# Adaptive-LN mixer kernel: four modulation rows as two pairs in 32-column strips of TensorE

## The chip, the cores and the metric

One core of one Trainium2 chip runs the whole program. The metric is the device time of one execution in microseconds; a time given for a kernel is the median of several runs. The profile is of one execution of its own, and its times count from the first instruction.

## The reference, cut to what matters

A token mixer (a 2-D real FFT filter) and a channel MLP, each behind a layer norm that a condition vector `c` modulates, and the whole backward pass:

```python
mod = (silu(c) @ w_mod).reshape(1, 6, 1, 1024)
sa, ca, ga, sb, cb, gb = six rows of mod
h = layernorm(x) * (1 + ca) + sa
x = x + ga * A(h, w_r, w_i)            # irfft2(rfft2(h) * (w_r + i w_i))
h = layernorm(x) * (1 + cb) + sb
x = x + gb * B(h, w1, b1, w2, b2)      # layernorm, 1024 -> 3584, gelu, 3584 -> 1024
outputs: x, and the gradients of A_x, w_r, w_i, w1, b1, w2, b2, c, w_mod for a given grad_out
```

`x` and `grad_out` are 2048 tokens of 1024 (bf16), `w_mod` is 1024 x 6144. The six rows of `mod` are what the change touches: row 0 is `sa`, 1 `ca`, 2 `ga`, 3 `sb`, 4 `cb`, 5 `gb`.

## The kernel before, in words

The program is written with a framework that places instructions on the engines, puts each engine's instructions into one fixed order by priorities and an estimate of their times, and adds the semaphores. An engine then works strictly in that order. Program order is the base of the priorities, so work written later is drawn forward as filler where an engine would otherwise stand, as far as its inputs are there. `tc.issue_after(ins)` makes what is written in its block follow `ins` on the same engine; `tc.high_priority()` puts evictions of PSUM first; `nc.any.tensor_copy` lets the framework choose ScalarE or VectorE.

**Modulation rows.** `u_b` (L255) holds silu(c), each of its 1024 values repeated over 128 columns. `mod_block(r, h)` (L272) makes one half (512 columns) of row r: it loads a tile `wblk` of w_mod of 1 MB (128 partitions x 8 pieces of 512 columns, L270, on SyncE's DMA queue), runs eight matmuls of 128x128 weights from `u_b` with 128x512 of `wblk` (L278) into one PSUM buffer, and copies the result, which then stands in all 128 partitions alike, to the row's place in SBUF (L281). For rows 1 and 4 it adds 1 (L283). The tiles go round a ring of three (`mod_tile`, L264, tags px3, px4, px5). PSUM has two buffers of the tag "s" (`ps_s`), two of "d" (`ps_d`) and four of "f" (`ps_f`); mod_block takes from "s".

**Order around the rows.** Row 1 and row 5 come first, their loads between those of x and grad_out (L358 to L374). Row 5 becomes the columns `gb_col` through eight tiny matmuls (L378), and scales grad_out while it is transposed by TensorE (L386) into `gBoT` (L390 VectorE, L394 ScalarE). Row 0 follows (L780), then the making of the Fourier matrices (`gen_mats`), and the fold of row 0 into `saf` (L791, L792). Then come six early "ph blocks": `ph_part(fc, ...)` (L802) makes one of 28 blocks of grad_out @ w2.T, in 32 matmuls (L808), copies them out (L814) and stores them (L816). Its weights come transposed through `load_w2t` (L340) into two slots of `wt`. Rows 2, 3 and 4 are placed behind the fourth and the sixth early ph block, three half rows each (`late_mods`, L819 to L827).

VectorE and ScalarE meanwhile normalize x, multiply it by row 1 and fold it into `fbuf` (L829 to L846; `saf` is added in L846). The forward spectral part (`spectral_core`, L867) starts with matmuls L535 on `fbuf`. Its last step `consume_fwd` (L851) uses rows 2, 3 and 4 and stores the inputs of the MLP. The other 22 ph blocks are written behind the spectral part (L883) and serve it as filler. Then z blocks (L937, the first MLP layer and gelu) and b passes (L994, the second layer) follow in a plan written out by hand (L1030), then the backward pass. Two forms used elsewhere are named by the prediction: `strip_sum` (L216), sums over partitions with 32-column weights into one of four 32-partition strips of a PSUM buffer, and L983, four matmuls with one row each at partitions 0, 32, 64 and 96 with `tile_position`.

The change's diff has no other function; the pair temporaries of the spectral part use px2 to px5 after the ring has ended.

Of the kernel before, what the change touches and what calls it, by code (L numbers as in the profile page):

```python
# [11 lines left out]
BF16 = mybir.dt.bfloat16  # L12
# [5 lines left out]
P = 128  # L18
S = 2048
D = 1024  # L20
F = 3584
NT = S // P
NDC = D // P
NFC = F // P
KH = D // 2
# [10 lines left out]
def kernel(  # L36
# [24 lines left out]
    nc = tc.nc  # L61
# [11 lines left out]
    def ps_s(name):  # L73
        return psum.tile([P, 512], FP32, tag="s", name=name)
# [185 lines left out]
    sar = reg.tile([P, 2, 1, D], BF16, name="sar", tag="gm")  # L260
# [3 lines left out]
    def mod_tile():  # L264
        wring[0] += 1
        return reg.tile([P, NDC, KH], BF16, name="wblk", tag=PXT[3 + wring[0] % 3])

    def mod_load(r, h, wblk, eng):
        cb = 2 * r + h
        eng.dma_start(out=wblk, in_=w_mod[:, cb * KH:(cb + 1) * KH].rearrange("(j p) n -> p j n", p=P))  # L270

    def mod_block(r, h, wblk=None):  # L272
        if wblk is None:
            wblk = mod_tile()[:]
            mod_load(r, h, wblk, nc.sync)
        pm = ps_s("pm")
        for jc in range(NDC):
            nc.tensor.matmul(pm[:], lhsT=u_b[:, jc, :], rhs=wblk[:, jc, :], start=(jc == 0), stop=(jc == NDC - 1))  # L278
        dst = MOD_DST[r][:, h * KH:(h + 1) * KH]
        with tc.high_priority():  # L280
            nc.any.tensor_copy(out=dst, in_=pm[:])  # L281
        if r in (1, 4):
            nc.vector.tensor_scalar(out=dst, in0=dst, scalar1=1.0, scalar2=None, op0=ALU.add)  # L283

# [67 lines left out]
    wm = {}  # L352

    def mod_get(r, h):
        wm[r, h] = mod_tile()
        mod_load(r, h, wm[r, h][:], nc.sync)
# [14 lines left out]
    for h in range(2):  # L371
        mod_block(5, h, wm[5, h][:])
# [407 lines left out]
    for h in range(2):  # L780
        mod_block(0, h)
# [769 lines left out]
```

## Time and profile before

| | before |
|---|---|
| median of 3 runs | 1419.12 us (1417.3 to 1419.79) |
| span of the profiled execution | 1417.4 us; its own time isn't given apart, the span lies 1.7 us below the median |
| TensorE busy | 1367.5 us, 96%, 6839 matmuls in the records |
| VectorE busy | 1071.1 us, 76% |
| ScalarE busy | 745.6 us, 53% |
| GpSimd busy | 377.1 us, 27% |
| moved by DMA | 333.22 MB, mean 235 GB/s |
| modulation rows | 12 half rows, 93 of 96 matmuls in the records, 6.2 to 104 us |

How to read it: busy time of TensorE is the time in which a matmul is under way; matmuls overlap, so a single one lasts about 0.38 us and the next can start 0.22 us after it. What an engine cost at a place is therefore read from the start of one thing to the start of the next. A line in a view is named by its line of the kernel and by the tiles that it writes and reads (`pm<-wblk,u_b`). Idle time has the name of what ended it. A few records of matmuls are missing, so counts can be short by one or two.

### The profile page before, as it was taken

To read this page: it belongs to the slowest core of one execution; us is meant where nothing else is said; L and a number is where in the kernel's file an instruction comes from. 1 tells how busy PE (TensorE), PEld (TensorE's weight loads), DVE (VectorE), ACT (ScalarE), POOL (GpSimd) and SP (SyncE) were. 2 spreads that over 40 slices of the span, in tenths; PEclk is the share of its full clock that TensorE was granted. 3 is DMA by queue.
4 is the path that set the end of the run, shared out by engine and by line. 5 is a ranking of instruction groups with operands and counts; after the bars stand their busy time and mean duration, and the time that the engine had idled before them with its cause. 6 is when DMAs were issued, how large, how long until landed. Compare 5 with 4: busy or idle time off the path is not lost. (4 is left out here: it accounts for less than half of the span.)

```text
span 1417.4 us, 18569 instructions
## 1 busy us (share of the span) xinstructions
PE 1367.5 (96%) x6839; PEld 663.0 (47%) x6963; DVE 1071.1 (76%) x1503; ACT 745.6 (53%) x1063; POOL 377.1 (27%) x479
## 2 busy tenths in 40 slices
PE   5999999999999999999999999999999999999998
PEld 2545675444444444444444444344544565444443
DVE  5898889987698877886520788999488659898642
ACT  4775667667887765666315583343623445343211
POOL 5500623201112122212210011011367432322332
PEclk8899999999999999999999999999999999999999
DMA  9972647899688776687999399996699997666993
GB/s 330 304 226 72 181 137 226 261 277 348 239 235 267 231 252 233 200 275 232 292 287 233 115 271 319 210 298 193 191 279 281 242 242 207 189 180 182 288 261 118
DMA packets 356689, 333.22 MB, mean 235 GB/s; under 512 B 207578, under 2 KB 297200, under 8 KB 356470
## 3 DMA queue, kind: packets, MB, share of 16 engines
q1 hardware_dynamic: 319110, 205.61, 55.1%
q0 software_dynamic: 37488, 126.42, 25.7%
q8 instruction: 54, 0.88, 0.3%
q14 instruction: 37, 0.30, 0.1%
HBM read 166.77 MB, written 115.92 MB: 199 GB/s over the span
## 5 line engine op out<-in xcount | busy, mean ns | idle before, releaser
L808 PE MATMUL pp<-gBoT,wt 128*128 128x512 bf16 x874 | 196.3, 381 | 4.0 <-DMA wt<-in_B_w_dram 2.8
L1094 PE MATMUL pg<-w1T,gzr 128*128 128x512 bf16 x877 | 195.0, 379 | 3.7 <-ACT gn3b L1109 1.7
L1445 PE MATMUL gw1acc<-gzh,n3n 128*128 128x512 bf16 x877 | 194.1, 379 | 1.0
L1094 PEld LDWEIGHTS <-gzr 128*128 128x128 bf16 x896 | 86.4, 98 | 110.8 <-issue 7.9
L808 PEld LDWEIGHTS <-wt 128*128 128x128 bf16 x896 | 87.6, 98 | 107.5 <-DMA wt<-in_B_w_dram 3.3
L937 PEld LDWEIGHTS <-w 128*128 128x128 bf16 x896 | 87.1, 98 | 107.4 <-issue 2.7
L1445 PEld LDWEIGHTS <-n3n 128*128 128x128 bf16 x896 | 87.2, 98 | 105.2 <-issue 1.3
L937 PE MATMUL pz<-n3Ta,w 128*128 128x512 bf16 x439 | 98.2, 379 | 1.8 <-ACT gt L940 1.3
L937 PE MATMUL pz<-n3Tb,w 128*128 128x512 bf16 x436 | 98.0, 379 | 0.7 <-issue 0.2
L940 ACT ACTIVATE gt<-pz,b_col 128x512 bf16<-128x512 f32 x112 | 73.5, 684 | 38.1 <-PE pz L937 37.6
L994 PEld LDWEIGHTS <-hhA 128*128 128x128 bf16 x608 | 58.9, 98 | 73.4 <-issue 3.0
L1227 PE MATMUL gw2acc<-gB,hhsA 128*128 128x512 bf16 x406 | 91.2, 379 | 0.5
L1449 ACT CAST gwo<-gw1acc 128x512 bf16<-128x512 f32 x49 | 28.5, 582 | 111.0 <-PE gw1acc L1445 103.2
L194 DVE TENSOR_TENSOR gt<-gt,gt 128x2048 bf16<-128x2048 bf16 x56 | 68.5, 1224 | 20.6 <-ACT gt L953 19.4
L951 ACT ACTIVATE gt<-gt 128x2048 bf16<-128x2048 bf16 x28 | 53.5, 1910 | 55.1 <-DVE gt L194 55.1
L194 DVE TENSOR_TENSOR ct<-ct 128x2048 bf16<-128x2048 bf16 x68 | 80.8, 1217 | 1.4 <-DMA d_n<-ct 0.5
L1234 ACT CAST gwo<-gw2acc 128x512 bf16<-128x512 f32 x46 | 26.7, 582 | 101.0 <-PE gw2acc L1227 83.2
L1227 PEld LDWEIGHTS <-hhsA 128*128 128x128 bf16 x416 | 40.6, 98 | 47.9
L947 ACT ACTIVATE gt<-gt 128x2048 bf16<-128x2048 bf16 x28 | 53.5, 1910 | 1.7 <-DVE w2sA L194 1.0
L1450 POOL DMA_DIRECT2D out_dram<-gwo x56 | 30.7, 549 | 88.6 <-ACT gwo L1449 66.2
L953 ACT ACTIVATE gt<-gt 128x2048 bf16<-128x2048 bf16 x28 | 53.4, 1908 | 0.4
L814 ACT CAST pho<-pp 128x512 bf16<-128x512 f32 x59 | 33.5, 582 | 32.4 <-PE pp L808 31.9
(346 smaller groups left out, 2544.5 us busy)
## 6 DMA issues: line engine op xcount, KB each, us to landing
gzr<-d_gz SPq DMA_DIRECT2D x28, 512.0 KB, 6.4
wblk<-in_w_mod_dram SPq DMA_DIRECT2D x12, 1024.0 KB, 8.8
out_dram<-otl POOLq DMA_DIRECT2D x48, 256.0 KB, 4.5
out_dram<-gwo POOLq DMA_DIRECT2D x96, 128.0 KB, 4.2
d_ph<-pho POOLq DMA_DIRECT2D x21, 512.0 KB, 5.6
d_hh<-hhA POOLq DMA_DIRECT2D x19, 512.0 KB, 5.0
w<-in_B_w_dram SPq DMA_DIRECT2D x7, 1024.0 KB, 11.7
hhC<-d_ph SPq DMA_DIRECT2D x14, 512.0 KB, 9.5
```

Of the source, the lines that this page charges most:

```text
L194: return nc.vector.tensor_tensor(out=out, in0=a, in1=b, op=op)
L808: last_pe[0] = nc.tensor.matmul(pp[:], lhsT=wt[:, fg % 2, cch, k * P:(k + 1) * P], rhs=gBoT[j][:, cch, :], start=(cch == 0), stop=(cch == ...
L814: nc.any.tensor_copy(out=ov, in_=pv)
L937: last_pe[0] = nc.tensor.matmul(pz[:], lhsT=w1s[g][:, cch, k * P:(k + 1) * P], rhs=n3T[:, cch, :], start=(cch == 0), stop=(cch == NDC - 1))
L940: z_in = nc.scalar.activation(out=zb[:, k, :], in_=pz[:], func=ACT.Identity, bias=b1_col[:, fc:fc + 1], scale=1.0)
L947: nc.scalar.activation(out=av, in_=zb, func=ACT.Square)
L951: nc.scalar.activation(out=sg, in_=bv, func=ACT.Sigmoid, scale=2.0 * GK)
L953: nc.scalar.activation(out=bv, in_=bv, func=ACT.Sigmoid, scale=-2.0 * GK)
L994: last_pe[0] = nc.tensor.matmul(pbs[i][:], lhsT=hh[:, k, i * P:(i + 1) * P], rhs=wp[:, k, :], start=False, stop=(g == 6 and k == 3))
L1094: last_pg[0] = nc.tensor.matmul(pgs[i][:], lhsT=gzs[b, g][:, k, i * P:(i + 1) * P], rhs=w1Ts[g][:, k, h * KH:(h + 1) * KH], start=(g == 0 ...
L1227: nc.tensor.matmul(acc[:], lhsT=hh_of(fc)[:, t, :], rhs=gBs[t // 4][:, t % 4, h * KH:(h + 1) * KH], start=(t == 0), stop=(t == NT - 1))
L1445: nc.tensor.matmul(acc[:], lhsT=n3ns[t // 4][:, t % 4, cch * P:(cch + 1) * P], rhs=gz2[t // 8][:, t % 8, :], start=(t == 0), stop=(t == NT ...
```

## The change

Rows 1 and 5 are made from two loads of a whole row each, now one for each half of the 1024 contraction rows (`mod_get(r, jh)`, 4 pieces of 1024 columns per partition), and use two PSUM buffers at once (`mod_row`); their matmuls are as many and as large as before.

Rows 0 and 2, and rows 3 and 4, are made as pairs (`mod_pair`). The weights are 32 columns of `u_b`, and the four half rows of a pair are accumulated in the four 32-partition strips of one PSUM buffer: 4 strips x 8 contraction blocks of 128x512. The buffer is copied to `strips` in SBUF, then four matmuls with a weight of one row of ones (at partitions 0, 32, 64 and 96) spread each strip's first row to all 128 partitions, into four PSUM buffers ("d", "d", "s", "s"), which are copied to the rows' places as before. Row 2 moves from behind the early ph blocks to the place of row 0; rows 3 and 4 stand behind the fourth early ph block, none behind the sixth. The ring of three tiles stays, and a pair loads four tiles, two for each half of the contraction.

```diff
-    sar = reg.tile([P, 2, 1, D], BF16, name="sar", tag="gm")
+    sar = reg.tile([P, 3, 1, D], BF16, name="sar", tag="gm")
+    strips = sar[:, 2, 0, :]
...
-    def mod_tile():
-    def mod_load(r, h, wblk, eng):
-    def mod_block(r, h, wblk=None):
+    def mod_get(r, jh):
         wring[0] += 1
+        wblk = reg.tile([P, 4, D], BF16, name="wblk", tag=PXT[3 + wring[0] % 3])
+        nc.sync.dma_start(out=wblk[:], in_=w_mod[jh * KH:(jh + 1) * KH, r * D:(r + 1) * D].rearrange("(j p) n -> p j n", p=P))
+        return wblk
+
+    def mod_out(r, h, pm):
         dst = MOD_DST[r][:, h * KH:(h + 1) * KH]
         with tc.high_priority():
             nc.any.tensor_copy(out=dst, in_=pm[:])
         if r in (1, 4):
             nc.vector.tensor_scalar(out=dst, in0=dst, scalar1=1.0, scalar2=None, op0=ALU.add)
+
+    def mod_row(r, wblks):
+        pms = [ps_s("pm") for _ in range(2)]
+        for jh in range(2):
+            for h in range(2):
+                for j in range(4):
+                    nc.tensor.matmul(pms[h][:], lhsT=u_b[:, 4 * jh + j, :], rhs=wblks[jh][:, j, h * KH:(h + 1) * KH],
+                                     start=(jh == 0 and j == 0), stop=(jh == 1 and j == 3))
+        for h in range(2):
+            mod_out(r, h, pms[h])
+
+    def mod_pair(n, rows):
+        pm = ps_s("pm")
+        for jh in range(2):
+            wblks = [mod_get(r, jh) for r in rows]
+            for j in range(4):
+                for k in range(4):
+                    nc.tensor.matmul(pm[32 * k:32 * (k + 1), :], lhsT=u_b[:, 4 * jh + j, 0:32],
+                                     rhs=wblks[k // 2][:, j, k % 2 * KH:(k % 2 + 1) * KH],
+                                     start=(jh == 0 and j == 0), stop=(jh == 1 and j == 3))
+        row4 = strips[:, n * KH:(n + 1) * KH]
+        with tc.high_priority():
+            nc.any.tensor_copy(out=row4, in_=pm[:])
+        pbs = [(ps_d, ps_s)[k // 2]("pmb") for k in range(4)]
+        for k in range(4):
+            nc.tensor.matmul(pbs[k][:], lhsT=ones_bf[32 * k:32 * k + 1, :], rhs=row4[32 * k:32 * k + 1, :], start=True, stop=True,
+                             tile_position=(32 * k, 0))
+        for k in range(4):
+            mod_out(rows[k // 2], k % 2, pbs[k])
...
-    mod_get(1, 0)
+    wm1 = [mod_get(1, 0)]
     load_tok(x4s[0], A_x, 0)
-    mod_get(1, 1)
-    mod_get(5, 0)
-    for h in range(2):
-        mod_block(1, h, wm[1, h][:])
-    mod_get(5, 1)
+    wm1.append(mod_get(1, 1))
+    wm5 = [mod_get(5, 0)]
+    mod_row(1, wm1)
+    wm5.append(mod_get(5, 1))
...
-    for h in range(2):
-        mod_block(5, h, wm[5, h][:])
+    mod_row(5, wm5)
...
-    for h in range(2):
-        mod_block(0, h)
+    mod_pair(0, (0, 2))
     gen_mats()
...
-    late_mods = [(r, h) for r in (2, 3, 4) for h in range(2)]
     for fc in range(PH_EARLY):
         ph_part(fc, (0, 1, 2, 3))
         if fc % 2 == 1:
             load_w2t(fc // 2 + 2)
-            if fc > 1:
+            if fc == 3:
                 with tc.issue_after(last_pe[0].ins):
-                    for r, h in late_mods[3 * (fc // 2 - 1):3 * (fc // 2)]:
-                        mod_block(r, h)
+                    mod_pair(1, (3, 4))
```

More of the change, by code (lines that the diff above doesn't have):

```diff
@@ L259 @@
     sb_row, saf = sb_saf[:, 0, :], sb_saf[:, 1, :]
-    sar = reg.tile([P, 2, 1, D], BF16, name="sar", tag="gm")
+    sar = reg.tile([P, 3, 1, D], BF16, name="sar", tag="gm")
+    strips = sar[:, 2, 0, :]
     MOD_DST = {0: sar[:, 0, 0, :], 1: opca_row, 2: ga_row, 3: sb_row, 4: opcb_row, 5: gb_row}
     wring = [0]
-    def mod_tile():
+    def mod_get(r, jh):
         wring[0] += 1
-        return reg.tile([P, NDC, KH], BF16, name="wblk", tag=PXT[3 + wring[0] % 3])
-    def mod_load(r, h, wblk, eng):
-        cb = 2 * r + h
-        eng.dma_start(out=wblk, in_=w_mod[:, cb * KH:(cb + 1) * KH].rearrange("(j p) n -> p j n", p=P))
-    def mod_block(r, h, wblk=None):
[L273 to L278, printed above, removed]
+        wblk = reg.tile([P, 4, D], BF16, name="wblk", tag=PXT[3 + wring[0] % 3])
+        nc.sync.dma_start(out=wblk[:], in_=w_mod[jh * KH:(jh + 1) * KH, r * D:(r + 1) * D].rearrange("(j p) n -> p j n", p=P))
+        return wblk
+    def mod_out(r, h, pm):
         dst = MOD_DST[r][:, h * KH:(h + 1) * KH]
@@ L350, in load_go @@
         nc.sync.dma_start(out=gos[j], in_=go_f[j * BW:(j + 1) * BW, :].rearrange("(a p) d -> p a d", p=P))
[L352 to L356, printed above, removed]
-    mod_get(1, 0)
-    load_tok(x4s[0], A_x, 0)
-    mod_get(1, 1)
-    mod_get(5, 0)
-    for h in range(2):
-        mod_block(1, h, wm[1, h][:])
-    mod_get(5, 1)
+    wm1 = [mod_get(1, 0)]
+    load_tok(x4s[0], A_x, 0)
+    wm1.append(mod_get(1, 1))
+    wm5 = [mod_get(5, 0)]
+    mod_row(1, wm1)
+    wm5.append(mod_get(5, 1))
     load_go(0)
```

## The prediction, made before the changed kernel was run

> **What bounds the kernel now.** I read the page's busy times first, then each engine in the stretches around the edited rows, then TensorE's own order of time. The stretches are cut where TensorE's work changes: loads and transposes to 44 us, the first ph blocks and six rows' halves to 122, the forward spectral part to 220, the remaining ph blocks to 325. Columns after the engines' busy time and (count): granted clock, DMA share, GB/s.
>
> ```profile
> PE 1367.5 (96%) x6839; PEld 663.0 (47%) x6963; DVE 1071.1 (76%) x1503; ACT 745.6 (53%) x1063; POOL 377.1 (27%) x479
> ```
> ```profile
> 44.00:122.00 78.00, 72.98 (x334) 32.76 (x339) 74.55 (x112) 52.42 (x77) 23.56 (x28) 1.00 0.70 222
> 122.00:220.00 98.00, 96.29 (x667) 65.46 (x675) 81.22 (x106) 66.76 (x117) 38.14 (x31) 1.00 0.51 150
> 220.00:325.00 105.00, 101.63 (x458) 45.76 (x466) 97.47 (x145) 67.04 (x100) 22.23 (x26) 0.98 0.91 263
> ```
>
> TensorE is nearly full in all three stretches, though VectorE is as full in the first and third. The order of time says which one sets the end. Its columns are start, length to the last end, engine, line, count, and in brackets the idle time before with its releaser.
>
> ```profile
> 49.61 1.89 PE L278 MATMUL pm<-wblk,u_b 128*128 128x512 bf16 x8
> 51.34 1.46 PE L808 MATMUL pp<-gBoT,wt 128*128 128x512 bf16 x6
> 52.63 1.89 PE L278 MATMUL pm<-wblk,u_b 128*128 128x512 bf16 x8
> 54.45 0.22 PE L209 MATMUL ptr<-ident,gb_bf 128*8 128x128 bf16 x1
> ...
> 76.14 3.62 PE L278 MATMUL pm<-wblk,u_b 128*128 128x512 bf16 x15
> 81.64 1.89 PE L278 MATMUL pm<-wblk,u_b 128*128 128x512 bf16 x8 [1.89 <-ACT rows L281]
> 83.36 13.98 PE L808 MATMUL pp<-gBoT,wt 128*128 128x512 bf16 x63
> 97.17 3.62 PE L278 MATMUL pm<-wblk,u_b 128*128 128x512 bf16 x16
> 102.17 1.89 PE L278 MATMUL pm<-wblk,u_b 128*128 128x512 bf16 x7 [1.38 <-DVE sb_saf L281]
> 103.90 0.27 PE L535 MATMUL pu<-smA,fbuf 128*128 128x256 bf16 x1
> ...
> 104.98 15.92 PE L808 MATMUL pp<-gBoT,wt 128*128 128x512 bf16 x72
> 122.16 0.83 PE L535 MATMUL pu<-smA,fbuf 128*128 128x256 bf16 x6 [1.26 <-DVE fbuf L194]
> ```
> ```profile
> 220.27 86.28 PE L808 MATMUL pp<-gBoT,wt 128*128 128x512 bf16 x392
> ...
> 324.84 7.07 PE L937 MATMUL pz<-n3Ta,w 128*128 128x512 bf16 x32
> ```
>
> The spectral part starts at 122.16, when VectorE delivers fbuf, so work saved before that point doesn't bring it forward. But TensorE isn't idle until then: it draws ph blocks (L808) forward as filler. After the spectral part 392 ph matmuls in a row are left, and block z begins at 324.84 with no wait at all. So TensorE's total work from 44 to 325 sets when z starts: time saved at 50 to 104 becomes filler, shortens the run after 220, and pulls z and what follows forward. **That is where the change is priced.**
>
> **The change, part by part.** *Removed:* rows 0, 2, 3 and 4, eight blocks of eight full matmuls. From each first start to the next other work: 1.73 (49.61 to 51.34), 1.82 (52.63 to 54.45), 7.22 (76.14 to 83.36), 6.73 (97.17 to 103.90), together **17.5 us** of TensorE. In it are 3.3 us of waits (1.89 and 1.38): a third block in a row needs one of two PSUM buffers back. Some records are missing (x15, x7), the starts aren't.
>
> *Added, strips:* two pairs, each two halves of 16 matmuls into four strips of 32 columns. This kernel has the form already, in sums of gradients:
>
> ```profile
> 959.70 5.78 PE L1227 MATMUL gw2acc<-gB,hht 128*128 128x512 bf16 x26
> 965.40 0.39 PE L217 MATMUL acc3a<-gn3b,ones_bf 128*32 128x512 bf16 x2
> 965.43 0.39 PE L217 MATMUL acc3a<-pru,ones_bf 128*32 128x512 bf16 x2
> ...
> 966.09 0.38 PE L217 MATMUL acc3a<-pru,ones_bf 128*32 128x512 bf16 x2
> 966.40 3.84 PE L1227 MATMUL gw2acc<-gB,hht 128*128 128x512 bf16 x16
> ```
>
> Sixteen strip matmuls take 1.00 us from first start to the next full matmul (965.40 to 966.40), not 16 × 0.216 (1.73 / 8) = 3.5: four run side by side. Entering costs a little: the last full one began about 965.10 (959.70 + 5.78 − 0.38), 0.30 before the strips instead of 0.22. So 1.08 a half, **4.3 us** for four halves. Here the weights differ from j to j, there they are all ones; both load them for every matmul, so I take the row.
>
> By the Trainium skill, page "TensorEngine Tiling (Array Packing)", section Key Properties, a change of tiling mode drains TensorE, which speaks against short tiled clumps. With a drain of about 0.16 us (a matmul of 0.38 that isn't overlapped by the next at 0.22; an estimate) at twelve changes this would be 2.0 us, and the forecast about 1 us later; the row shows some of it, inside the 1.00 and the 0.08.
>
> *Added, spreads:* twice four one-row matmuls at row strips, the form of L983:
>
> ```profile
> 364.77 1.67 PE L937 MATMUL pz<-n3Ta,w 128*128 128x512 bf16 x6
> 366.37 0.39 PE L983 MATMUL pbo<-b_row,ones_bf 1*128 1x512 bf16 x4
> 366.70 3.63 PE L994 MATMUL pbo<-w2sA,hhB 128*128 128x512 bf16 x16
> ```
>
> 0.33 us from start to start, and 0.09 at entry (last pz at about 364.77 + 1.67 − 0.38 = 366.06): 0.42 each, **0.8 us**.
>
> *Added wait:* the spreads read the evicted strips, so TensorE, which works in its fixed order, stands for the eviction unless filler was put between; queued behind it are ph matmuls and the transposes at 54. The eviction:
>
> ```profile
> L281 ACT CAST rows<-pm x5: 563/568/585, 9.6 to 104.3; 128x512 bf16<-128x512 f32 x5
> L281 DVE CAST rows<-pm x3: 682/691/692, 21.8 to 83.8; 128x512 bf16<-128x512 f32 x3
> ```
>
> Between nothing (ph matmuls cover it) and 1.9 a pair, the longer of the two waits for an eviction above. I take the shorter, 1.4, since both engines are full there: **2.8 us**. Evictions go from eight to ten, 0.57 on ScalarE or 0.69 on VectorE each. VectorE's part can move 122.16 by up to 1.4 us; filler covers that on TensorE. Without it, it would be paid in full.
>
> *Moved, loads:* still twelve of 1 MB, now with 2 KB pieces instead of 1 KB, and the ring of three tiles is used four at a time. So each pair's fourth load waits until the pair's first half is multiplied.
>
> ```profile
> 42.42 12.49 SPq L270 DMA_DIRECT2D wblk<-in_w_mod_dram  x5
> ...
> 78.49 5.43 SPq L270 DMA_DIRECT2D wblk<-in_w_mod_dram  x3
> ```
> ```profile
> PE pm L278 <- DMA wblk<-in_w_mod_dram: 10.8, 4, 5.1
> ```
> ```profile
> DMA to landing us min/median/max: 8.8/8.8/10.6
> ```
> ```profile
> 24.15 1.90 PE L278 MATMUL pm<-wblk,u_b 128*128 128x512 bf16 x7 [0.57 <-DMA wblk<-in_w_mod_dram]
> ```
>
> The last of the four waits for these loads (10.8 us in all, the longest 5.1) ends at 24.15; the eight blocks after 44 wait for none. For the fourth load: zero if 9 to 11 us of ph blocks stand between the halves, up to 10.6 if none do. Even after the fourth early ph block 64 ph matmuls (13.8 us) of the six are left to stand there, so I take zero. Behind that load SyncE's queue holds the spectral weights (63 us) and the next ph weights; today it stands for ring tiles in the same two places, so nothing for that. Row 0 completes some 10 us later than at 55 (a load's landing), but its fold, saf, is added only at 96:
>
> ```profile
> 96.17 0.69 DVE L194 TENSOR_TENSOR fbuf<-fbuf,sb_saf 128x1024 bf16<-128x1024 bf16 x1
> ```
>
> *Rows 1 and 5* keep their 32 full matmuls; the second load still ends each, eight matmuls follow it as before, two evictions come together on two engines: nothing. The pieces' size shows in two stretches where DMA is full, 50 to 60 us (mostly 1 KB pieces) and 30 to 40 (mostly larger):
>
> ```profile
> DMA packets 2969, 3.77 MB, mean 377 GB/s; under 512 B 79, under 2 KB 2711, under 8 KB 2966
> ```
> ```profile
> DMA packets 1920, 3.99 MB, mean 399 GB/s; under 512 B 109, under 2 KB 109, under 8 KB 1918
> ```
>
> The first four loads (4 MB in the DMA-bound start) would pass in 10.5 instead of 11.1 us: 0 to 0.6, I take **0.3**. By the Trainium skill, page "DMA: Bandwidth & Descriptors", section Specifications, line rate is reached from 512 B on; by that it is nothing.
>
> *Given back:* with z some 9 us earlier, VectorE's and ScalarE's tail of the spectral part, set from 122.16, doesn't move with it, and both meet in 315 to 395, where DMA and ScalarE are near full:
>
> ```profile
> 325.00:335.00 10.00, 9.95 (x48) 4.50 (x47) 3.31 (x6) 9.16 (x12) 0.00 (x0) 1.00 1.06 385
> ...
> 375.00:385.00 10.00, 9.95 (x47) 4.50 (x47) 6.56 (x6) 10.00 (x10) 0.75 (x1) 1.00 0.45 158
> ```
> ```profile
> PE pp L808 <- DMA wt<-in_B_w_dram: 2.8, 1, 2.8
> ```
> ```profile
> 392.38 2.97 PE L937 MATMUL pz<-n3Ta,w 128*128 128x512 bf16 x13 [1.33 <-ACT gt L940]
> ```
>
> Two waits stand there today, for ph weights (2.8) and ScalarE (1.33). I take **1.0** more; the bounds are 0 and the whole gain.
>
> **Sum:** −17.5 + 4.3 + 0.8 + 2.8 − 0.3 + 1.0 = **−8.9 us**. The profiled span is 1417.4 us, so 1408.5 for such an execution; the median of three runs is 1419.12, 1.7 above the span, so **1410.2** against it.
>
> **Rivals.** (1) *Given back at z*: waits for w1, ph weights or ScalarE between 300 and 395 eat 3 to 6 us; for it speak the full DMA and the ScalarE wait above, against it VectorE's idle two thirds at 325 to 335. About 1414.5. (2) *Slower: the fourth load is exposed.* Place: TensorE between the halves of a pair. If the halves stand with no filler between, each pair waits about 9.5 us (8.8 landing to 10.6), and both give −8.9 + 19 = +10, 1429. It decides once the exposed waits pass 9 us: one pair alone ends at about 1420, no change. For it: the ring holds three tiles, the order is fixed beforehand, and a load at a full DMA can be later than planned. Against it: none of the eight blocks waits today. (3) *The strips don't run together* because their weights change: 64 × 0.216 = 13.8 instead of 4.3, so −8.9 + 9.5 = +0.6, 1420. The row at 965.40 speaks against it.
>
> **How the numbers follow.** Forecast (1406 to 1412.5): 0.55. Rival 1: 0.19, still faster. One pair exposed, rival 3, or the whole gain handed back: 0.13, no change. Both exposed: 0.13. So faster by over 0.2% (2.8 us, about what a measurement of this kernel can tell from no change) 0.74, within it 0.13, slower 0.13. Low end: no eviction waits (−2.8), nothing given back (−1.0): 1406.4, so 1406. High end: up to one exposed load, 1421; beyond it lies mostly rival 2.
>
> **What would show it.** Right: strip clumps of 16 about 1.0 us long; four spreads in about 0.4; more than 72 ph matmuls before the spectral start; some 45 fewer after 220; z begins near 316; spectral start within 2 us of 122. Wrong: TensorE waiting for wblk after 44 us, an eviction wait over 2 us before a spread, z no earlier than 321, or new waits for w, wt or gt up to 400.

## The result, and the profile after

The changed kernel takes **1432.19 us** (median of 4 runs, 1428.68 to 1433.61), the kernel before 1418.21 beside it (4 runs, 1417.23 to 1419.79): a ratio of **1.0092, 95% interval 1.0078 to 1.0105**, slower by 13 to 14 us. The forecast was 1410.2, faster. The profiled execution of the changed kernel took 1428.68, with a span of 1426.9. It is the fastest of its four, so its trace shows 9.5 us of the loss.

The page of after, busy times:

```profile
PE 1362.2 (95%) x6848; PEld 658.3 (46%) x6971; DVE 1072.7 (75%) x1505; ACT 745.2 (52%) x1063; POOL 374.0 (26%) x479
```

TensorE is busy 5 us less (1367.5 before), and the program is longer. TensorE in order of time, changed kernel, the same stretch as was shown of before:

```profile
48.49 0.39 PE L294 MATMUL pm<-wblk,u_b 128*32 128x512 bf16 x2 [1.71 <-DMA wblk<-in_w_mod_dram]
...
52.45 1.04 PE L294 MATMUL pm<-wblk,u_b 128*32 128x512 bf16 x14 [0.65 <-DMA wblk<-in_w_mod_dram]
...
61.62 1.88 PE L294 MATMUL pm<-wblk,u_b 128*32 128x512 bf16 x14 [2.64 <-DMA wblk<-in_w_mod_dram]
63.44 2.05 PE L821 MATMUL pp<-gBoT,wt 128*128 128x512 bf16 x5
65.42 0.40 PE L302 MATMUL pmb<-sar,ones_bf 1*128 1x512 bf16 x4
...
90.51 1.04 PE L294 MATMUL pm<-wblk,u_b 128*32 128x512 bf16 x14 [2.92 <-DMA wblk<-in_w_mod_dram]
91.48 1.04 PE L821 MATMUL pp<-gBoT,wt 128*128 128x512 bf16 x4
92.45 0.39 PE L302 MATMUL pmb<-sar,ones_bf 1*128 1x512 bf16 x4
...
102.99 24.12 PE L821 MATMUL pp<-gBoT,wt 128*128 128x512 bf16 x109
128.32 0.83 PE L549 MATMUL pu<-smA,fbuf 128*128 128x256 bf16 x6 [1.21 <-DVE fbuf L194]
...
227.44 73.76 PE L821 MATMUL pp<-gBoT,wt 128*128 128x512 bf16 x335
311.55 17.02 PE L821 MATMUL pp<-gBoT,wt 128*128 128x512 bf16 x70 [10.34 <-DVE pho L827]
328.41 6.85 PE L948 MATMUL pz<-n3Ta,w 128*128 128x512 bf16 x31
```

Strips and spreads are as forecast: 14 strip matmuls in 1.04 us, four spreads in 0.39 (the 1.88 stands right behind a wait; the granted clock from 61.6 to 63.5 was 0.52). TensorE waits for wblk four times (7.9 us together). The time it saved went into filler: 109 ph matmuls stand right before the spectral start, 72 before, and after 220 us some 405 are left instead of 454. But the **spectral start** comes at 128.32, not 122.16. And near 311 TensorE stands for 10.34 us and has lost all of its lead: z begins at 328.41, 3.6 later than before.

VectorE between 44 us and the spectral start, first before, then after (busy us, mean ns, then the idle time ahead of the group and what ended it):

```profile
L814 DVE CAST pho<-pp 128x512 bf16<-128x512 f32 x9 | 6.1, 680 | 0.0
L814 DVE CAST phr<-pp 128x512 bf16<-128x512 f32 x3 | 2.0, 680 | 0.0
```
```profile
L274 DVE CAST rows<-pmb 128x512 bf16<-128x512 f32 x2 | 1.4, 691 | 6.4 <-PE pmb L302 6.4
...
L827 DVE CAST pho<-pp 128x512 bf16<-128x512 f32 x13 | 8.9, 682 | 1.9 <-PE pp L821 1.9
L827 DVE CAST phr<-pp 128x512 bf16<-128x512 f32 x4 | 2.7, 678 | 0.5 <-issue 0.5
```

VectorE copies 17 ph blocks instead of 12 (3.5 us more), **stands 6.4 us for the spreads** (4.14 until 65.91 and 2.22 until 92.94) and 1.9 for ph blocks; for 0.5 more the profile shows no releaser. It reaches the spreads' copies in its fixed order just after TensorE's waits for a fourth wblk load (they end at 61.62 and 90.51), when the strips, their eviction and the spreads are still to come. The sums of the stretch, before to 122.2 and after to 128.3:

```profile
44.00:122.20 78.20, 73.02 (x335) 32.81 (x341) 74.66 (x112) 52.42 (x77) 23.56 (x28) 1.00 0.70 222
```
```profile
44.00:128.30 84.30, 74.12 (x373) 31.68 (x378) 74.76 (x109) 52.11 (x76) 16.58 (x25) 0.98 0.67 213
```

Its busy time is the same to 0.1 (the added ph copies are offset by work on gBoT, gidx and rows that lies elsewhere in the plan). Its idle time went from 3.5 to 9.5: that is the 6.1 us by which the spectral start is late. So in this kernel the start is late by standing, not by more work.

SyncE's queue near 290 and VectorE's wait there, changed kernel:

```profile
275.34 5.40 SPq L363 DMA_TRANSPOSE wt<-in_B_w_dram  x1
280.84 13.48 SPq L933 DMA_TRANSPOSE n3Ta<-d_n  x1
294.50 1.19 SPq L890 DMA_DIRECT2D w<-in_B_w_dram  x2
295.78 8.23 SPq L363 DMA_TRANSPOSE wt<-in_B_w_dram  x1
304.12 0.53 SPq L876 DMA_DIRECT2D d_n<-ct  x1
304.81 0.38 SPq L890 DMA_DIRECT2D w<-in_B_w_dram  x1
314.79 1.95 SPq L363 DMA_TRANSPOSE wt<-in_B_w_dram  x1
```
```profile
309.67 1.22 DVE L194 TENSOR_TENSOR ct<-ct 128x2048 bf16<-128x2048 bf16 x1 [12.21 <-DMA d_n<-ct]
```

The chain: a d_n store (304.12) stands in SyncE's queue behind the transposing loads of n3Ta and wt; VectorE stands 12.21 us until that store has read its tile; behind VectorE stand the ph evictions, and behind them TensorE (10.34). Before, SyncE had passed the same store at 289.65, ahead of that wt load:

```profile
281.87 4.38 SPq L922 DMA_TRANSPOSE n3Ta<-d_n  x1
286.43 0.46 SPq L879 DMA_DIRECT2D w<-in_B_w_dram  x1
289.65 0.38 SPq L865 DMA_DIRECT2D d_n<-ct  x1
290.08 0.90 SPq L879 DMA_DIRECT2D w<-in_B_w_dram  x1
292.77 8.78 SPq L341 DMA_TRANSPOSE wt<-in_B_w_dram  x1
```

Of the 9.5 us of these two executions, 3.6 are there when z starts. Another 4.0 come by the first b pass (366.4 before, 374.0 after): z waits for ScalarE's gt, and the 15 matmuls behind that wait ran at a granted clock of 0.68 (368.7 to 374.0) and took 5.30 us, where 0.22 each would make some 3.4:

```profile
368.74 5.30 PE L948 MATMUL pz<-n3Ta,w 128*128 128x512 bf16 x15 [2.18 <-ACT gt L951]
```

Most of the rest lies between 742 and 954, where the longest wait for gn3a is 3.5 us instead of 0.9.

### The profile page after: what moved, and what is told of

It is laid out like the page before. It is cut to its first block, busy times and chain, and to the rows that moved or that the text cites. A ratio compares the mean times of both kernels' runs of the same rounds, so it can differ in the third digit from the quotient of the medians.

```text
span 1426.9 us, 18600 instructions
## 1 busy us (share of the span) xinstructions
PE 1362.2 (95%) x6848; PEld 658.3 (46%) x6971; DVE 1072.7 (75%) x1505; ACT 745.2 (52%) x1063; POOL 374.0 (26%) x479
## 5 line engine op out<-in xcount | busy, mean ns | idle before, releaser
L1105 PEld LDWEIGHTS <-gzr 128*128 128x128 bf16 x896 | 87.1, 98 | 114.2 <-issue 12.9
L1238 PE MATMUL gw2acc<-gB,otl 128*128 128x512 bf16 x219 | 49.4, 379 | 0.4 <-issue 0.2
## 6 DMA issues: line engine op xcount, KB each, us to landing
out_dram<-gwo POOLq DMA_DIRECT2D x96, 128.0 KB
```

What stands on the lines that cost most here:

```text
L1105: last_pg[0] = nc.tensor.matmul(pgs[i][:], lhsT=gzs[b, g][:, k, i * P:(i + 1) * P], rhs=w1Ts[g][:, k, h * KH:(h + 1) * KH], start=(g == 0 ...
L1238: nc.tensor.matmul(acc[:], lhsT=hh_of(fc)[:, t, :], rhs=gBs[t // 4][:, t % 4, h * KH:(h + 1) * KH], start=(t == 0), stop=(t == NT - 1))
```

## The experiments

Theory after the result: the saved TensorE time isn't lost in the strips but has nowhere to go. VectorE's chain sets the spectral start, ph blocks drawn forward lengthen it, and SyncE's order near 290 turns the delay into a wait. Rivals: the prediction's own (TensorE's total work sets z), and that strips, spreads or the larger loads cost in themselves. Ratios are against the kernel before, run beside each; S is the spectral start in the profiled execution, z the start of block z.

| kernel | us, median | ratio, 95% interval | S | z |
|---|---|---|---|---|
| before | 1417.4 to 1420.1 | 1 | 122.2 | 324.8 |
| after | 1432.2 | 1.0092, 1.0078 to 1.0105 | 128.3 | 328.4 |
| e_rows | 1422.6 | 1.0030, 1.0005 to 1.0054 | 118.2 | 325.1 |
| e_full | 1418.6 | 1.0011, 0.9996 to 1.0026 | 117.4 | 322.0 |
| e_act | 1434.0 | 1.0107, 1.0087 to 1.0127 | 129.5 | 334.1 |
| e_four | 1432.0 | 1.0107, 1.0088 to 1.0126 | 124.0 | 325.1 |
| b_cut | 1440.6 | 1.0168, 1.0142 to 1.0193 | 129.2 | 331.7 |
| c_phs | 1422.1 | 1.0023, 1.0006 to 1.0040 | 120.2 | 320.6 |
| b_vec | 1445.5 | 1.0185, 1.0153 to 1.0217 | 128.0 | 337.7 |
| b_dbl | 1444.3 | 1.0168, 1.0126 to 1.0210 | 119.6 | 347.1 |
| b_phs | 1424.6 | 1.0035, 1.0012 to 1.0059 | 121.3 | 325.9 |
| f_phs | 1427.9 | 1.0077, 1.0053 to 1.0100 | 123.3 | 327.7 |
| a_phs | 1431.3 | 1.0095, 1.0068 to 1.0121 | 126.6 | 329.4 |
| a_ord | 1428.7 | 1.0072, 1.0049 to 1.0095 | 129.7 | 332.7 |
| b_ord | 1423.6 | 1.0042, 1.0025 to 1.0060 | 121.7 | 326.6 |
| a_dn | 1428.9 | 1.0078, 1.0047 to 1.0109 | 129.3 | 330.9 |
| a_wt | 1424.6 | 1.0032, 1.0015 to 1.0049 | 127.8 | 326.0 |
| a_n3 | 1428.0 | 1.0058, 1.0037 to 1.0080 | 132.3 | 331.1 |
| g_late | 1444.4 | 1.0178, 1.0130 to 1.0227 | 125.8 | 342.2 |
| g_all | 1433.0 | 1.0099, 1.0063 to 1.0135 | 124.8 | 333.0 |

S and z are of one execution each; executions of one kernel differ by up to 12 us (g_late, 1439.1 to 1451.0), and those shown of e_four, b_cut and b_vec are their fastest, that of a_n3 its slowest. Nor is z the whole of a loss: e_four starts z 0.3 us later than before and its span is 8.3 longer (1425.7), b_cut 6.8 and 17.0 (1434.4), and c_phs starts z 4.2 earlier and is 5.1 longer (1422.5).

### The change taken apart

**e_rows**: only the whole-row loads are kept; all rows are made by full matmuls at the places of before (but row 3's first half stands behind the sixth early ph block, not the fourth).

```diff
-    mod_pair(0, (0, 2))
+    mod_row(0, [mod_get(0, jh) for jh in range(2)])
...
+                    for r in ((2,), (3, 4))[fc // 2 - 1]:
+                        mod_row(r, [mod_get(r, jh) for jh in range(2)])
```

> Every row is made by full matmuls from two whole-row loads (2 KB pieces), rows 0 and then 2, 3 and 4 at the places of the kernel before: the new loads alone, no strips, no spreads. Theory (two standstills: VectorE stands for the late pairs and starts the spectral part 6 us late; the store of d_n stands behind a transposing load in SyncE's queue and costs TensorE 10 us): none of the two is here, ph blocks begin some 2 us earlier, so 1415 to 1419. Rival (the whole-row loads themselves cost): 1424 or more.

Measured 1422.6, between the two expectations. By the ratio the loads' new form costs about a third of the loss, with an interval from almost nothing to over half of it; S is 4 us earlier than before and z isn't.

**e_full**: places, loads and ring of the changed kernel, but 64 full matmuls into four buffers, no strips, no spreads.

```diff
-                    nc.tensor.matmul(pm[32 * k:32 * (k + 1), :], lhsT=u_b[:, 4 * jh + j, 0:32],
+                    nc.tensor.matmul(pbs[k][:], lhsT=u_b[:, 4 * jh + j, :],
```

> The pairs keep their place, their loads, the ring of three and the four PSUM buffers, but the weights are 128 columns wide: 64 full matmuls, no strips buffer, no spreads. Theory: TensorE gets 9 us of work back, VectorE still stands for the fourth load's rows (spectral start 126 to 130), the store of d_n is ahead of the transposing load in SyncE's order as in the kernel before, so the 10 us wait is gone: 1421 to 1428. Rival (the strips and spreads themselves are what costs): 1419 or less.

Measured 1418.6, below what the theory gave and where its rival, that strips and spreads cost in themselves, had put it: with some 9 us *more* TensorE work the whole loss is gone, so neither the places nor the loads carry it. But four things are gone here at once: the strips, the spreads, the time they save, and the changed kernel's order in SyncE's queue near 290 (it is that of before again). VectorE copies 10 ph blocks there before S, which is at 117.44:

```profile
117.44 0.83 PE L542 MATMUL pu<-smA,fbuf 128*128 128x256 bf16 x6 [1.20 <-DVE fbuf L194]
```

**e_act**: the strips' and spreads' evictions on ScalarE. **e_four**: a tile of its own for each pair's fourth load.

```diff
-            nc.any.tensor_copy(out=dst, in_=pm[:])
+            nc.scalar.copy(out=dst, in_=pm[:])
```
```diff
-            wblks = [mod_get(r, jh) for r in rows]
+            wblks = [mod_get(r, jh, PXT[1 - n] if jh and r == rows[1] else None) for r in rows]
```

> The changed kernel with all evictions of the pairs (strips and spreads) on ScalarE, so nothing in VectorE's order waits for a spread but the adding of 1 for row 4. SyncE's order comes out with the second store of d_n ahead of the transposing load. Theory: spectral start at 122 to 124 instead of 128, no 10 us wait near 300, so 1411 to 1419. Rival (the late fourth load costs through TensorE alone, or the strips do): 1427 or more, spectral start still near 128.

> The changed kernel with a tile of its own for each pair's fourth load (the place of grad_out's first block for the first pair, of the index buffer for the second), so no load waits for the pair's first half. SyncE's order keeps the second store of d_n behind the transposing load. Theory: TensorE's waits for wblk after 44 us fall from 7.9 to under 3, VectorE's for the spreads from 6.4 to under 2.5, spectral start 122 to 125, but the 10 us wait near 300 stays: 1423 to 1429. Rival (the fourth load is the whole loss): 1410 to 1416.

Both theories missed: 1434.0 and S at 129.5 are what e_act's rival had given, and 1432.0 is above both ranges of e_four. In e_act VectorE no longer stands for spreads but for ph blocks (8.83 us once), since TensorE stood 6.87 for the fourth load. In e_four the waits for wblk fell to 3.4, S came to 124.0, and 6.40 us of waiting for wt stood near 305 all the same. Taking one wait away moves it to the next.

### Is it the strips, or the time they save?

**b_cut** leaves out TensorE work in the kernel before; **c_phs** adds one edit to it.

```diff
+        nj = NDC if r in (1, 5) else 1
-        for jc in range(NDC):
+        for jc in range(nj):
```
```diff
-                nc.any.tensor_copy(out=ov, in_=pv)
+                (nc.scalar.copy if fc < 10 else nc.any.tensor_copy)(out=ov, in_=pv)
```

> The kernel before, in which rows 0, 2, 3 and 4 multiply only the first of their eight chunks of 128 inputs: 8 matmuls instead of 64, so these four rows hold only an eighth of their sum. All loads and all evictions stay. TensorE has 56 x 0.216 = 12.1 us less to do between 49 and 105 us, with no strips, no spreads, no pairs. If TensorE's total work sets the start of z (the prediction's step), z begins near 313 instead of 324.8 and the time is near 1406. If VectorE's chain and SyncE's queue hold the end of the ph blocks, z begins no earlier than 320, TensorE shows 6 to 12 us of new waits before its last ph blocks (for wt, or for a ph eviction), and the time is 1413 to 1421.

> The kernel of b_cut (rows 0, 2, 3 and 4 multiply only the first of their eight chunks, so they hold an eighth of their sum) with one more edit: the evictions of ph blocks 0 to 9 are given to ScalarE instead of to whichever of two engines is planned. In b_cut VectorE does 15 of them before the spectral start (10.2 us) and stands 3.6 us for pm. Theory: TensorE time freed before the spectral start is filled with ph blocks, their evictions lengthen VectorE's chain, and that chain sets the spectral start and z. Then the spectral start goes from 129.2 to 114 to 122, z from 331.7 to 316 to 325, and the time from 1440 to 1410 to 1425. Rival: SyncE's order of ph weights holds z whatever VectorE does: the spectral start may move, but TensorE waits 10 us or more near 310, z is past 327 and the time 1430 or more.

b_cut is the sharpest result: 12.1 us less TensorE work, no strip in it, and the kernel is **23 us slower**, outside both expectations (SyncE's planned order is another one there too). VectorE's ph copies ahead of S there, the sums of the stretch (columns as above), S, and the wait that follows:

```profile
L815 DVE CAST pho<-pp 128x512 bf16<-128x512 f32 x11 | 7.5, 685 | 0.1
L815 DVE CAST phr<-pp 128x512 bf16<-128x512 f32 x4 | 2.7, 678 | 0.0
```
```profile
44.00:129.20 85.20, 78.28 (x356) 34.45 (x354) 77.35 (x114) 54.93 (x82) 23.39 (x30) 0.98 0.77 229
```
```profile
129.17 0.83 PE L536 MATMUL pu<-smA,fbuf 128*128 128x256 bf16 x6 [1.12 <-DVE fbuf L194]
...
315.29 16.53 PE L809 MATMUL pp<-gBoT,wt 128*128 128x512 bf16 x64 [15.89 <-DMA wt<-in_B_w_dram]
```

Against before, VectorE has 2.7 us more work ahead of S and stands 4.3 us more (85.20 − 77.35 against 78.20 − 74.66); for pm, the rows' PSUM buffers, it stands 3.6. After S the chain of the changed kernel shows again: VectorE stands 24.8 us for a d_n store.

c_phs is edited in nothing but who copies the ph blocks, and SyncE's order from the first d_n store to the first load of hhC is the same in both traces: S goes to 120.22 and the time to 1422.1, so 18.5 of the 23 us come back. So SyncE's order alone doesn't make b_cut's loss; VectorE's load ahead of S carries most of it. That the copies drawn forward by the freed time carry it isn't shown, since c_phs takes all 15 copies away and only three are more than before. And c_phs, with 12 us less TensorE work and S earlier than before, is still not faster than before: it waits 7.07 for wt near 300, and one wait of 4.59 for gt near 392 eats z's lead of 4 us.

**b_vec** lengthens VectorE's chain alone, **b_dbl** TensorE's work alone (the loop of b_cut with `2 * NDC`, chunks taken modulo NDC).

```diff
         tt(fb, fb, bcn(opca_row, 4), ALU.mult)
+        for _ in range(3 if i == 3 else 0):
+            tt(x4, fb, fb, ALU.add)
```

> The kernel before with 6.9 us more on VectorE and nothing else: three extra sums of the size 128x4096 (2.3 us each, as L194's are) in the last chunk ahead of the spectral start, into a tile that is overwritten later. TensorE's work is untouched and the planned order puts 31 ph matmuls (6.7 us) more ahead of the spectral start. If TensorE's total work sets z, as the prediction has it, the filler takes up the delay: spectral start 129, z within 1 us of 324.8, time 1418 to 1421. If VectorE's chain from the spectral start sets what follows: spectral start 129, TensorE stands 4 us or more for a ph eviction or a ph weight near 310, z 328 to 332, time 1424 to 1433, as in the changed kernel, though no row was touched.

> The kernel before, in which rows 0, 2, 3 and 4 run each of their 64 matmuls twice, so that these rows hold twice their sum: 64 x 0.216 = 13.8 us more TensorE work before 122 us, no more loads, no more evictions. If TensorE's work sets z: z near 338 and the time near 1432. If the kernel is held by VectorE's chain alone: z within 2 us of 324.8, 1418 to 1421. If both are close to balance in the kernel before, as the small wait of 2.8 us for ph weights there suggests: fewer ph blocks before the spectral start give VectorE back some 5 us there, TensorE's queue of ph blocks becomes the longer one, z 331 to 338, time 1425 to 1432.

By the prediction's step b_vec would have cost nothing. It cost **25 us**, more than its own 6.9 and than the other theory's 6 to 15; TensorE's order ahead of S is that of before but for 31 more ph matmuls, and SyncE's near 290 but for one w1 load that passes ahead of the d_n store:

```profile
127.95 0.83 PE L535 MATMUL pu<-smA,fbuf 128*128 128x256 bf16 x6 [1.55 <-DVE fbuf L194]
...
296.66 16.69 PE L808 MATMUL pp<-gBoT,wt 128*128 128x512 bf16 x64 [4.49 <-DMA wt<-in_B_w_dram]
319.51 10.34 PE L808 MATMUL pp<-gBoT,wt 128*128 128x512 bf16 x40 [6.16 <-DMA wt<-in_B_w_dram]
```

b_dbl cost 24 for 13.8, beyond all three expectations, with S at 119.6 and a wait of 9.9 for wt. So the kernel before stands near balance: more work on either engine ahead of S costs more than itself. Part of the difference appears as waits for ph weights at 290 to 340, where the planned order of SyncE is another one each time, and part behind the start of z (12.9 us later in b_vec, of 20.8 in its span). How much of that is the added work and how much the new order, these two runs don't separate.

**a_phs, b_phs, f_phs**: the edit of c_phs in the kernel of e_act, in the kernel before, and in that of e_full.

> The changed kernel with the evictions of ph blocks 0 to 9, of the strips and of the spreads given to ScalarE, so that VectorE neither copies ph blocks (17 x 0.68 = 11.6 us before the spectral start) nor stands for spreads (6.4 us). Theory: the spectral start goes from 128.3 to 112 to 120, z from 328.4 to 316 to 324, the time from 1432 to 1412 to 1421. Rival, SyncE's order or the late fourth load holds it: a wait of 8 us or more for wt or wblk, 1427 or more. It could also fall short because ScalarE, with 10 us more, delivers its part of fbuf late: then VectorE waits for ScalarE before the spectral start.

> The kernel before with the same one edit, evictions of ph blocks 0 to 9 on ScalarE; the control for the two others. VectorE loses 12 x 0.68 = 8.2 us before the spectral start, which goes from 122.2 to 113 to 117. TensorE's work is that of before, and its queue of ph blocks now decides: z 320 to 325, time 1413 to 1419. If the spectral start alone set z, z would be near 318 and the time near 1411.

> The pairs with full 128-column weights and four buffers instead of strips and spreads (the kernel of e_full), with the same edit, evictions of ph blocks 0 to 9 on ScalarE. Against a_phs it tells what strips and spreads are worth when VectorE's chain is clear. Spectral start 110 to 115, z 319 to 324, time 1413 to 1419. If a_phs is 4 us or more faster than this, the strips' saved TensorE time reaches the end once VectorE's chain is clear; if they are equal within 3 us or a_phs is slower, another thing holds z.

All three theories missed, on the slow side; a_phs did as its rivals said (a wait of 8.84 for wt, and a late ScalarE). The copies left VectorE, but ScalarE delivers its half of fbuf late. What VectorE waits for, ahead of S, in a_phs:

```profile
DVE fbuf L194 <- ACT fbuf L526: 9.3, 2, 5.8
DVE rows L276 <- ACT rows L274: 4.3, 1, 4.3
```

ScalarE works in order as well, and stands 11.3 us for ph blocks and 4.0 for strips of a TensorE that waits for wblk (8.3 us). In f_phs VectorE waits 9.5 for the same fbuf. a_phs is 3.4 us slower than f_phs, so by the test set for f_phs the strips' saved time doesn't reach the end there either. So neither engine has room for the copies here: the edit that gained 18.5 us on b_cut loses some 5 in the kernel before.

### SyncE's order

**a_ord** and **b_ord** exchange the order of SyncE's ph weights, w1 loads, n3Ta and d_n stores between the two kernels; TensorE's order stays. **a_dn** issues the d_n stores from GpSimd. **a_wt** queues n3Ta behind the thirteenth ph-weight load; the planner then puts the d_n store ahead of n3Ta. **a_n3** makes n3Ta a plain load and so leaves out its transposition.

```diff
+                for one, two in zip(chain, chain[1:]):
+                    behind(two, one)
```
```diff
-        nc.sync.dma_start(out=chunk_rows(d_n3, i), in_=tmp)
+        nc.gpsimd.dma_start(out=chunk_rows(d_n3, i), in_=tmp)
```
```diff
-            with tc.issue_after(w2ts[11].ins) if b == 0 else ExitStack():
+            with tc.issue_after(w2ts[12].ins) if b == 0 else ExitStack():
```

> The changed kernel with one thing undone: between 230 and 320 us SyncE issues its ph weights, its w1 loads, its n3Ta and its d_n stores in the order of before, so that the second d_n store stands ahead of the thirteenth ph-weight load and not behind it. TensorE's order of matmuls is the same as in the changed kernel. If SyncE's order makes the 10.3 us wait of TensorE near 311 (VectorE stands 12.2 us for the d_n store, and the ph evictions stand behind it), that wait falls under 4 us, z begins at 318 to 323, and the time is 1419 to 1425. If the late spectral start (128.3 us) alone holds z, through the d_n rows that come some 5 us later, the wait only goes to another load: z at 327 or later, time 1429 to 1433. If the strips and spreads themselves cost it: as the changed kernel, 1432.

> The kernel before with one thing changed: SyncE issues these same loads and stores in the order of the changed kernel (second d_n store behind the thirteenth ph-weight load, two w1 loads behind n3Ta). TensorE's order is that of before, nothing of the modulation rows is touched. If this order is what costs, TensorE shows a wait of 6 to 10 us near 300 to 312 that before has not, z begins 3 to 8 us later than 324.8, and the time is 1421 to 1427. If the late spectral start is needed for it, nothing happens: 1417 to 1420.

> The changed kernel with its four d_n stores issued by GpSimd and not by SyncE, so that they stand behind no ph-weight load. If SyncE's order costs, VectorE's wait for the d_n store (12.2 us) is gone, TensorE's longest wait before its last ph blocks is under 6 us, z begins at 319 to 325, and the time is 1419 to 1427. If the late spectral start holds z, 1429 to 1433. It can also get worse, if GpSimd reaches the issue late because of its own work: then the wait for d_n stays.

> The changed kernel with n3Ta queued behind the thirteenth ph-weight load instead of the twelfth, so that the ph weights that TensorE needs next don't stand behind it, and the second d_n store moves ahead of n3Ta with it; TensorE's order unchanged. Theory: the thirteenth load lands some 10 us earlier, the 10.3 us wait falls under 4 us; n3Ta then lands near 310, which z can bear, and the fourteenth ph-weight load stands behind n3Ta and may cost 0 to 6 us: z 319 to 326, time 1416 to 1428. Rival, VectorE's chain holds z: 1428 to 1433. It is the one form of these that could be a better kernel, if it ends under 1417.

> The changed kernel in which the first n3Ta load (the one of block 0, d_n into n3Ta) is a plain load of the same 1 MB instead of a transposing one, so n3Ta holds the rows in another layout and block 0's products are of wrong values; order of every queue and of TensorE as in the changed kernel. Theory: between 265 and 330 us the transposing loads of n3Ta and of the ph weights fill the DMA engines and SyncE's queue one after the other (n3Ta alone 13.5 us in the changed kernel, 4.4 before), and the ph weights behind it come late. Then SyncE passes n3Ta in under 3 us, TensorE's 10.3 us wait before the last ph blocks falls under 4, z begins at 316 to 322, and the time is 1413 to 1423. Rival: VectorE's later chain from 128.3 us holds z by itself; then the wait stays or goes to d_n or to a ph eviction, z 326 or later, 1428 to 1433.

b_ord held in its time: the order alone, with no row touched, costs the kernel before some 6 us, though by a smaller wait than expected (2.84 for a ph eviction near 310, z 1.8 later), so most of it lies behind the start of z. a_wt held: S is as late as in the changed kernel (127.8) and the ratio falls from 1.0092 to 1.0032, so **two thirds of the loss go when these loads are moved in SyncE's queue**. That isn't the share that the changed kernel's own order costs: the order of before (a_ord) brings back a fifth, to 1.0072, and a_wt's order was not tried in the kernel before. SyncE in a_wt; the d_n store passes at 293.69, not 304.12, and n3Ta needs 8.69:

```profile
274.81 16.31 SPq L363 DMA_TRANSPOSE wt<-in_B_w_dram  x2
293.69 0.40 SPq L876 DMA_DIRECT2D d_n<-ct  x1
294.32 0.60 SPq L890 DMA_DIRECT2D w<-in_B_w_dram  x1
294.98 8.69 SPq L933 DMA_TRANSPOSE n3Ta<-d_n  x1
303.77 1.15 SPq L890 DMA_DIRECT2D w<-in_B_w_dram  x2
305.01 9.20 SPq L363 DMA_TRANSPOSE wt<-in_B_w_dram  x1
```

VectorE's long wait is gone; TensorE waits 6.36 for the fourteenth wt load instead of 10.34. a_ord and a_dn ended at 1428.7 and 1428.9, about where the late S by itself had been expected to hold them: in a_dn the wait is still 10.56, now for wt itself, so freeing the d_n store alone does little. a_n3 (1428.0) speaks against n3Ta's transposing as the cause: n3Ta passes in 0.67 us, but the two w1 loads behind it then take the time, and wt is issued at 295.56, in the changed kernel at 295.78:

```profile
285.05 0.67 SPq L934 DMA_DIRECT2D n3Ta<-d_n  x1
285.90 9.56 SPq L890 DMA_DIRECT2D w<-in_B_w_dram  x2
295.56 9.96 SPq L363 DMA_TRANSPOSE wt<-in_B_w_dram  x1
```

So most of n3Ta's 13.5 us isn't its own transposing: with the two w1 loads it held the queue for 14.9 us there (280.84 to 295.78) and for 10.5 here. Whatever is next in SyncE's queue takes that time, which suggests that it waits for the loads issued earlier; that isn't shown further.

### Two attempts at a better kernel

**g_late** moves the spreads behind the second pair with their copies on ScalarE; **g_all** adds e_four's tiles and the chain of a_ord.

```diff
-            mod_out(rows[k // 2], k % 2, pbs[k])
+            nc.scalar.activation(out=MOD_DST[r][:, h * KH:(h + 1) * KH], in_=pbs[k][:], func=ACT.Identity,
+                                 bias=one_col[:, 0:1] if r == 4 else 0.0, scale=1.0)
...
+        if i == 3:
+            with tc.issue_after(last_pe[0].ins):
+                mod_spread(row4s[0], (0, 2))
+                mod_spread(row4s[1], (3, 4))
```

> The changed kernel with the spreads moved: both pairs' spreads follow the second pair, with four rows' copies on ScalarE (row 4's plus one in the same instruction), the strips' evictions on ScalarE, and the fold of row 0 and its two sums go ahead of the last chunk. So VectorE never stands for a spread (6.4 us in the changed kernel); the loads and strips are as in the changed kernel. Theory: spectral start 116 to 122 instead of 128.3, z 317 to 324, time 1411 to 1420. If the spectral start stays past 125 because the in-order engines stand for ph blocks while TensorE waits for the fourth load, 1424 to 1432.

> As g_late, with a tile of its own for each pair's fourth load (as in e_four), and SyncE's order of ph weights, w1 loads, n3Ta and d_n stores held to that of before (as in a_ord). All three named costs are taken away: spectral start 115 to 121, no wait of over 4 us for ph weights, z 315 to 322, time 1408 to 1417. If it ends at 1418 or more although the spectral start is before 121, what is given back lies behind z, with VectorE and ScalarE.

Both missed widely: 1444.4 and 1433.0. In g_late VectorE stands for no spread, but 5.64 us for a ph block, behind the second pair's third load, for which TensorE waited 4.00:

```profile
82.30 0.61 PE L296 MATMUL pm<-wblk,u_b 128*32 128x512 bf16 x2 [4.00 <-DMA wblk<-in_w_mod_dram]
82.84 7.94 PE L826 MATMUL pp<-gBoT,wt 128*128 128x512 bf16 x24
```

SyncE's n3Ta there takes 19.43 us, and TensorE waits 18.0 for ph weights in all. g_all cured the wblk waits (3.0 in all) and still waits 16.0 for ph weights. No kernel here beats before; e_full equals it.

## Why the prediction was wrong

**The step that failed** is the one on which all was priced: "So TensorE's total work from 44 to 325 sets when z starts: time saved at 50 to 104 becomes filler, shortens the run after 220, and pulls z and what follows forward." The first half came true (109 filler matmuls before S, some 50 fewer after 220). The second didn't. I read that z began with no wait and took TensorE for the bound, though the quoted stretches showed VectorE as full, 74.55 of 78 and 97.47 of 105 us. b_cut (less TensorE work, slower) and b_vec (only VectorE's work edited, slower) show it, and c_phs too, which has b_cut's order of SyncE, 12 us less TensorE work and S 2 us earlier than before, and is not faster; b_dbl shows that TensorE isn't free either. Both engines were near their limit. In the changed kernel VectorE lost the 6 us by standing, most of it for the spreads; the copies of the filler drawn forward added 3.5, for which other work left the stretch.

**By the terms.** *Strips and spreads* were right (1.04 for 14; 0.39 for four). *Eviction waits, 2.8 on TensorE*: TensorE had filler there and no wait stands before a spread; the wait fell on VectorE, which stood 6.4 us for the spreads, and that side was not in the sum. "VectorE's part can move 122.16 by up to 1.4 us" was too small by 5, and "filler covers that on TensorE" was the same failed step. *The fourth load*, taken at zero, left TensorE waiting 2.64 and 2.92 us, each followed by VectorE's wait of 4.14 or 2.22 for the spreads behind. *Loads' pieces, −0.3*: ph blocks start at 42.1 instead of 44.4, more than taken (41.6 to 42.8 in the thirteen kernels with the new loads, 43.0 to 44.4 in the seven with the old), and none of it reaches the end. *Given back, 1.0 with the whole gain as bound*: the loss went beyond that bound. All was given back near 305, and 4.0 us more between 328 and 374, where z waits for gt; the first through a queue (SyncE's d_n store behind a ph-weight load) that the prediction had looked at for wblk only and not followed through VectorE to the ph evictions.

**By the rivals.** The slower side was there, but by another mechanism: waits of 9.5 us per pair on TensorE between halves. They were 2.6 and 2.9; the loss comes by way of VectorE and SyncE. Rival 1 named the right stretch (300 to 395) with the wrong size, and not the wait for a ph eviction that was the longest there. Rival 3 is excluded by the strips' time.

**What stays open.** How the 13 us divide isn't settled. a_wt leaves some 4.5 (ratio 1.0032), with S as late as in the changed kernel and a wait of 6.36 for wt. e_four has little waiting for wblk and S at 124.0, and is as slow as the changed kernel. No run has strips without spreads, and none has strips together with an S before 122, so what they would be worth then was not measured. Nor is it settled why 7 to 14 us of added work became 24 or 25 in b_vec and b_dbl. A rival to all of it was not excluded: nearly every edit also gave a new planned order, and none of the 19 edited kernels is faster than before, not even b_phs, whose TensorE work is that of before and whose S comes 0.9 us earlier; that the order of before happens to fit well would explain a part of each loss.

## What to carry to other kernels

A matmul engine that is 96% busy and starts the next stage without a wait isn't the bound by that, when its time is filled with work drawn forward: look for the engine that ends the stage without filler, and count what each piece of filler asks of it (here 0.68 us of VectorE for 1.73 us of TensorE). Follow a saved microsecond through every in-order queue that it passes, the copies and the DMA queue too, until it reaches the end. Before trusting such a saving, leave the work out entirely in one experiment: b_cut would have told at once that under this planning nothing was to be had.

## What the runs showed of the hardware

**A wait often costs more than its length.** After 10.34 us of standing, 70 ph matmuls took 17.02 us, 0.243 each against 0.220 in the 335 before (73.76): 1.6 more. In g_late 24 took 7.94 after a wait of 4.00, where 5.3 were due. It isn't so each time: after 2.92 us of standing 14 strip matmuls took their 1.04. The granted clock tells the same (the number ahead of the last two), first in the stretch 290 to 325 of before and of after, then behind g_late's wait:

```profile
290.00:325.00 35.00, 32.00 (x139) 14.07 (x141) 30.33 (x43) 20.76 (x29) 3.13 (x5) 0.95 1.10 293
```
```profile
290.00:325.00 35.00, 24.55 (x107) 10.86 (x108) 19.71 (x31) 14.61 (x20) 1.60 (x3) 0.85 1.01 287
```
```profile
82.30:91.00 8.70, 8.70 (x34) 3.20 (x37) 3.06 (x8) 3.03 (x4) 0.00 (x0) 0.67 1.02 238
```

The Trainium skill, page "TensorE: Matmul & The Clock Gate", section "Part 1: The HAM clock gate", says that TensorE falls to half its clock after at least one idle window of about 3.4 us and is released after at least one busy one. One window at half clock would lose 1.7 us, an estimate from that page's figure. The first case agrees with that; the second lost 2.6 by the records, and a granted clock of 0.67 over 8.7 us means half clock for some 5.7 of them, more than one window.

**The issuing queue stands, and for very different times.** SyncE's instruction for one and the same transposing load of n3Ta (1 MB) lasted from 4.38 us (before) over 13.48 (after) to 23.26 (b_cut); those for a ph-weight load of 0.5 MB lasted 1.87 to 8.78 in the kernel before, between 223 and 307 us. A plain load of n3Ta passed in 0.67, and the two w1 loads in its place took 9.56 (a_n3). A row that merges two ph-weight loads (16.31 us in a_wt) also holds the time between them: the two start 13.8 us apart there (274.8 and 288.6), which is what 64 ph matmuls take.
